# RWKV recurrence with a gated convolution behind it: plan lengths as measured, and stores from a buffer of their own

## The chip, the cores and the metric

The kernel runs on one core of one Trainium2 chip. The metric is the device time of one execution in microseconds; lower is better.

## The reference

The first half is a recurrence over 768 steps for 4 batches and 8 heads, with a 40 x 40 state each. The second half takes its output as 320 channels, runs a causal convolution of 5 taps, a sigmoid gate and two 320 x 320 matrix products. Everything is float32.

```python
for t in range(S):                                   # S = 768
    y[:, :, t] = einsum('bhd,bhde->bhe', r_t, state)
    Sa = einsum('bhde,bhe->bhd', state, a_t)
    state = state * w_t[:, :, None, :] - einsum('bhd,bhe->bhde', Sa, b_t) \
            + einsum('bhd,bhe->bhde', v_t, k_t)
x = y.transpose(0, 2, 1, 3).reshape(B, S, H * D)     # 4 x 768 x 320
gate = sigmoid(sum_k conv_w[k] * x shifted by 4 - k)
out = (gate * (x @ w_val)) @ w_out
```

## The kernel before

The sequence is cut into 24 chunks of 32 steps. All 32 pairs of batch and head are worked on together, packed into the partitions. A chunk has a part that doesn't need the state and a part that does.

Without the state: load the inputs (`load`), running products of the decay (`scan`, L351), their reciprocals (`ln`, `exp`, `nw0`, `nw1`), scaled inputs (`at`, `kt`), copies with zeros in the other half (`qb`, L380), the products between steps (`am`, L389) and their evacuation (`aev_l`, `aev_k`, L408). Four chunks share one triangular solve on VectorE: `begin`, 60 `step` operations (L443, L445) and `end` (L452); the first four chunks are solved by halves with `q1` and `q2` on TensorE, for which `end2` transposes a block into the tile `td`, and `db` spreads it.

With the state: `u0` (L515, L519), `evac_u0` (L523), `ut` (L528) and `u` (L532), their evacuations on ScalarE (`evac_ut` L536, `evac_u` L540), `g` (L544) and `evac_g` (L547), the output and the new state in PSUM (`ysa`, `ysb`, L553), from which `evac_s` (L563) takes the state and `evac_y` (L577) the output. `st` and `kbt` (L419) are transposes.

`evac_y` writes the output into a half of the tile XEW, one half for each pair of chunks in turn. `new_xe` (L572) copies the four steps before the pair into its half; it waits until the half's former content has been moved. From there the second half of the reference is done pair by pair (the last two chunks singly, in tiles that have come free):

- `xd`: twelve small transfers within the chip's memory (L705) that bring channels into the partitions, from xe to a half of the tile XTW, called xt
- `cv`: the convolution, on ScalarE (first tap, L725) and VectorE (L727), into the one tile AG
- `abs`, `gexp`, `gln`, `max`, `gate`: the sigmoid, in AG
- `val` (L90, L98) and `gv` (L757): the value product and its multiplication with the gate, in AG
- `out` (L108): the output product; `os` (L772): its copy from PSUM into the same half of XTW; `store` (L776): the transfer to the output

The order of all this is not written by hand. Each operation is given to a planner as `op(name, engine, length, predecessors, function, delay, ...)`, with length and delay in ns. The delay is the time from the operation's end to when another engine can use its result; for a transfer it stands for the landing. The planner runs a greedy list scheduling forward and backward, several times, ranks operations by how long a chain hangs on each, and keeps the shortest plan. Every engine then gets its instructions in the plan's order, and waits at run time for what each really needs. The plan also decides where TensorE gets matmuls without use (L795) in planned gaps, and which of four PSUM slots a result takes.

The two stores of a pair and its moves are issued by POOL (the very last by SP). The moves wait, in the plan and at run time, for the stores of the pair two before, as these read the same half of XTW.

Of the kernel before, what the change touches and what calls it, by code (L numbers as in the profile page):

```python
# [17 lines left out]
C = 32  # L18
# [26 lines left out]
def ac(n):  # L45
    return 154 + 0.833 * n
# [106 lines left out]
class Plan:  # L153
# [111 lines left out]
def fast_path(ctx, tc, ins, out, nch, cst, wts, wz, wmx):  # L265
# [57 lines left out]
    def B2(nm, c):  # L323
        return (nm, c, 0), (nm, c, 1)
# [62 lines left out]
    def amat(c, s):  # L387
        for j, i in JI:
            T.matmul(out=s[hr(i), j * 64:j * 64 + 64], lhsT=QB[c % NQ][:, pj(j, i)].rearrange("p z t -> p (z t)"),  # L389
                     rhs=st_["kb", c][:, pj(j, i)].rearrange("p x t -> p (x t)"), start=True, stop=True)  # L390
# [24 lines left out]
    def flips(s, src, g, w):  # L415

        for b in range(4):
            u = 8 * g + 2 * b
            T.transpose(out=s[:, b * 128:b * 128 + ER], in_=src[:, u:u + 2].rearrange("p i f -> p (i f)"), identity=ident[0:ER, 0:ER])  # L419
# [38 lines left out]
                        in1=maskL.unsqueeze(1).to_broadcast([128, 8, C]), op=ALU.mult)  # L458

    def end2(g):  # L460
        td = st_["td", g] = ch.tile([128, P16, 4, 8], F32, name="td", bufs=1)
        V.transpose(out=td.rearrange("p s c u -> p (s c u)"), in_=st_["x", g][:, 0:P16].rearrange("p s t -> p (s t)"))

    def nblock(c, z):
# [114 lines left out]
    def slot(nm):  # L579
        return st_["slot", nm]  # L580

    for c in range(nch):
        q = c - NQ
        g, c4 = sof[c]
        op(("load", c), "SP", 4300, ["cst"] * (c == 1) + [(x, c - 3) for x in ("at", "kt", "relu", "scan")], lambda c=c: load(c), 2200)
# [15 lines left out]
        op(am, "PE", 870, [("qb", c, 0), ("qb", c, 1), ("kt", c), ("pre_a", q)] + gg + [("q2", sg[TWO][0] - 1)] * (c == NQ - 1), lambda c=c, n=am: amat(c, slot(n)), give=[("aev_l", c), ("aev_k", c)])  # L601
        op(("aev_l", c), "DVE" if two else "ACT", 480 if two else 604, [am, "cst", ("lz", g)] + gg, lambda c=c, n=am: aev_l(c, slot(n)))
        op(("aev_k", c), "DVE", 440, [am, ("pre_a", q)], lambda c=c, n=am: aev_k(c, slot(n)))
        op(("pre_a", c), "DVE", dv(512), [("aev_k", c), "cst", ("u0", c - 2)], lambda c=c: pre_a(c))
        for k in range(2):
            kt = ("kbt", c, k)
            op(kt, "PE", 430, [("kt", c), "cst", *B2("ysb", q)] + ([("q1", sg[TWO][0] - 2), ("q1", sg[TWO][0] - 1)] if NQ - 2 <= c < NQ else []), lambda c=c, k=k, n=kt: flips(slot(n), st_["kb", c].rearrange("p u x t -> p u (x t)"), k, 128), give=[("kbe", c, k)])
# [26 lines left out]
        op(("load2", c), "SP", 2500, [("load", 4 + c)] * (c < 2) + [*B2("ysb", c - 2), ("u0", c - 2)], lambda c=c: load2(c), 2200)  # L634
        op(("load3", c), "SP", 3200, [("load2", c)] + [("rs", c - 1), ("rs1", c - 1), ("vs", c - 1), ("es", c - 1)], lambda c=c: load3(c), 2200)
# [5 lines left out]
        op(("u0", c), "PE", 1900 if c else 900, [("pre_a", c), ("qb", c, 0), ("qb", c, 1), ("load2", c), *B2("evac_s", c - 1), *B2("evac_y", c - 1), "pz"], lambda c=c: stage_u0(c))  # L641
# [9 lines left out]
        op(nm, "PE", 960, [("evac_ut", c), ("rs", c), ("rs1", c), ("vs", c)], lambda c=c, n=nm: stage_g(c, slot(n)), give=[("evac_g", c)])  # L651
        op(("evac_g", c), "DVE", dv(512, 1), [nm, "cst", ("load2", c)], lambda c=c, n=nm: evac_g(c, slot(n)))
        fr = [("evac_u", c, 0), ("evac_u", c, 1), ("evac_ut", c)]
        if c:
            for k in range(2):
                op(("ysa", c, k), "PE", 650, fr + [("evac_st", c - 1, k), ("es", c)], lambda c=c, k=k: stage_y(c, k, S2, RE, 40, True, False))
        for k in range(2):
            op(("ysb", c, k), "PE", 650, fr + [("ysa", c, k), ("evac_g", c), ("kbe", c, k)], lambda c=c, k=k: stage_y(c, k, KB[c % NQ], st_["w", c], 64, c == 0, True))
            if c + 1 < nch:
                op(("evac_s", c, k), "DVE", dv(320, 1), [("ysb", c, k), ("u0", c), ("st", c - 1, k), "sz"], lambda c=c, k=k: evac_s(c, k))  # L660
            op(("evac_y", c, k), "DVE", dv(256, 1), [("ysb", c, k), ("xe", gof[c][0])], lambda c=c, k=k: evac_y(c, k))
            if c + 1 < nch:
                nm = ("st", c, k)
                op(nm, "PE", 430, [("evac_s", c, k), "cst", "sz"], lambda c=c, k=k, n=nm: flips(slot(n), ST, k, 104), give=[("evac_st", c, k)])
# [29 lines left out]
    for gi, (c, n) in enumerate(groups):  # L694
# [10 lines left out]
                (nc.sync if last and hf else G).dma_start(out=o, in_=i)  # L705
        last = tail > 0
        mq = ("SP", 860, 650) if last else ("POOL", 560, 850)
        xw = [x for j in range(n) for x in B2("evac_y", c + j)] + wl + [("cv", pg, 4, 0), ("cv", pg, 4, 1), ("cv", pg, 4, 2), ("val", pg, 2), ("store", pg, 0), ("store", pg, 1)]
# [54 lines left out]
        for j in range(n):  # L763
            def outm(j=j, c=c, n=n, gf=gf):
                out_mms(nc, slot(("out", c, j))[:, 0:DM], gf, wo, j, n)
            nm = ("out", c, j)
            op(nm, "PE", 1980, prev_gv + om + ([] if late else [when[3 + j]]), outm, give=[("os", c, j)])
            om = [nm]
            prev_out.append(nm)

            def osc(j=j, c=c, xo=xo):
                A.copy(out=xo[0][:, xo[1] + j * DM:xo[1] + (j + 1) * DM], in_=slot(("out", c, j))[:, 0:DM])  # L772
            op(("os", c, j), "ACT", ac(DM), om, osc)

            def store(j=j, c=c, n=n, L=L, xo=xo, last=last):
                (nc.sync if last else G).dma_start(out=out[j * B // n:(j + 1) * B // n, c * C:c * C + L], in_=xo[0][:, xo[1] + j * DM:xo[1] + (j + 1) * DM])  # L776
# [172 lines left out]
```

## Time and profile before

| | |
|---|---|
| median of 3 runs | 543.69 us (542.23 to 549.13) |
| profiled execution | 543.18 us |
| its span, first to last instruction | 541.3 us |
| time outside the span | 1.9 us |
| busy: TensorE, VectorE, ScalarE, POOL | 423.7, 378.6, 316.1, 103.4 us |
| mean granted TensorE clock | 0.852 |
| read from and written to HBM | 49.25 and 3.93 MB |

In rows of the profile, PE is TensorE, DVE VectorE, ACT ScalarE, POOL GpSimd, and SP the engine that issues loads. A row of the timeline has the start in us, the length, the engine, the line of the program, the operation, output and inputs by the program's names, the shape, how many, and in brackets the idle time of the engine before it with what ended it. A row of the chain has start, length and what was waited for; a row of the list of waits has the total in us, the number of times and the longest.

### The profile page before, as it was taken

Reading aid. Unit: us, or ns where it says so; the run is one execution under the profiler, and the core shown is the slowest. Engines: PE = TensorE matmul, PEld = TensorE weight load, DVE = VectorE, ACT = ScalarE, POOL = GpSimd, SP = SyncE. Lnnn points to the kernel's source line nnn. Section 1 sums busy time; section 2 is a strip of 40 time slices with the busy share of each in tenths; the row PEclk is TensorE's granted clock in tenths of the full one; section 3 lists DMA queues with packets and bytes.
Section 4 is the critical chain, followed back from the end, with each engine's and each line's share of the span. In section 5 each row is a group of like instructions: output and inputs, shape, how many; then the busy total and the mean of one; then the engine's idle time right before and its main releaser. Section 6 shows DMA issues by size and latency. Waiting matters only on the chain.

```text
span 541.3 us, 22177 instructions
## 1 busy us (share of the span) xinstructions
PE 423.7 (78%) x9769; PEld 364.2 (67%) x9769; DVE 378.6 (70%) x935; ACT 316.1 (58%) x644; POOL 103.4 (19%) x187
## 2 busy tenths in 40 slices
PE   4707669879769979897983996985987988998790
PEld 3707669778759768777872876774876766776660
DVE  4548946887999988796994695994795746443430
ACT  3636455657867769685684485676464527562530
POOL 3000000040310140032031023013014051338410
PEclk8766756888869999897996898997999697999696
DMA  8855733474664646647355526441252352341101
GB/s 179 199 134 135 188 85 90 100 172 111 152 152 99 146 118 136 154 112 164 86 130 133 145 49 154 87 113 29 78 105 60 66 124 59 96 90 35 37 17 38
DMA packets 24262, 58.96 MB, mean 109 GB/s; under 512 B 10953, under 2 KB 15215, under 8 KB 21665
## 3 DMA queue, kind: packets, MB, share of 16 engines
q1 hardware_dynamic: 13169, 49.52, 39.1%
q0 software_dynamic: 10992, 7.97, 6.3%
q8 instruction: 78, 1.28, 1.1%
q14 instruction: 23, 0.19, 0.1%
HBM read 49.25 MB, written 3.93 MB: 98 GB/s over the span
## 4 chain that ended last, share of the span: by engine, by line
PE 42%; DMA 18%; issue 17%; DVE 11%; ACT 6%; POOL 5%; POOLq 0%; ACTq 0%; DVEq 0%
DMA out<-xt 6%; PE pf L90 5%; PE pc L553 4%; PE pf L389 4%; DMA xt<-xe 4%; PE pf L108 4%; DMA ew<-in_ew 4%; PE pf L419 4%; PE pc L532 4%; PE pf L544 4%; POOL xt L705 4%; PE pc L515 3%; PE pc L519 3%; PE pc L528 3%; DMA ag<-in_wts 1%
## 5 line engine op out<-in xcount | busy, mean ns | idle before, releaser
L705 POOL DMA_DIRECT2D xt<-xe x132 | 68.0, 521 | 199.9 <-DVE tm L443 113.7
L727 DVE SCALAR_TENSOR_TENSOR ag<-xt,wts,ag 128x256 f32<-128x256 f32 (+1 forms) x132 | 53.6, 431 | 10.7 <-ACT ag L725 10.6
L776 POOL DMA_DIRECT2D out<-xt x22 | 18.2, 827 | 218.7 <-ACT xt L772 211.6
L389 PE MATMUL pf<-kb,qb 104*64 104x64 f32 x768 | 34.8, 260 | 30.7 <-DVE kb L384 22.8
L389 PEld LDWEIGHTS pf<-kb,qb 104*64 104x64 f32 x768 | 31.9, 172 | 33.0 <-ACT er L356 16.0
L445 DVE TENSOR_TENSOR x<-x,tm 128x58 f32<-128x58 f32 (+9 forms) x164 | 51.4, 314 | 0.6
L443 DVE TENSOR_TENSOR tm<-x 128x58 f32<-128x58 f32 (+9 forms) x164 | 51.3, 313 | 0.6
L108 PE MATMUL pf<-wts,ag 128*128 128x320 f32 x132 | 47.6, 482 | 1.0 <-DVE ag L757 1.0
L544 PE MATMUL pf<-rb,vu 104*64 104x64 f32 x768 | 33.0, 248 | 17.6 <-DVE ak L408 12.3
L544 PEld LDWEIGHTS pf<-rb,vu 104*64 104x64 f32 x768 | 29.2, 159 | 22.2 <-DVE ak L408 12.7
L540 ACT COPY w<-pc 32x640 f32<-32x640 f32 x48 | 32.9, 685 | 17.4 <-PE pc L532 16.9
L351 DVE TENSOR_TENSOR_SCAN lam<-ew,ind 104x528 f32<-104x528 f32 x24 | 30.0, 1248 | 16.8 <-DMA ew<-in_ew 16.7
L532 PE MATMUL pc<-ub,T 64*32 64x80 f32 x768 | 37.4, 254 | 5.3 <-issue 5.3
L553 PE MATMUL pc<-re,s 40*40 40x72 f32 x1472 | 33.1, 231 | 8.3 <-ACT s L422 4.6
L523 ACT ACTIVATE ub<-pc,cst 128x320 f32<-128x320 f32 x48 | 22.7, 522 | 28.0 <-PE pc L519 28.0
L532 PEld LDWEIGHTS pc<-ub,T 64*32 64x32 f32 x768 | 31.9, 121 | 7.8 <-issue 6.5
L380 ACT ACTIVATE qb<-qa,cst 104x512 f32<-104x512 f32 x48 | 32.5, 714 | 7.4 <-DVE qa L377 7.3
L503 ACT ACTIVATE rb<-rv,cst 104x512 f32<-104x512 f32 x48 | 34.5, 719 | 1.9 <-DMA rv<-in_rv 1.6
L553 PEld LDWEIGHTS pc<-re,s 40*40 40x40 f32 x1472 | 27.1, 117 | 12.5 <-ACT s L422 5.0
L553 PE MATMUL pc<-w,kbt 64*40 64x72 f32 x1536 | 33.3, 232 | 1.9 <-DVE w L547 1.1
L419 PE MATMUL pf<-cst,kb 104*128 104x104 f32 x192 | 28.7, 290 | 7.2 <-DVE kb L384 4.3
L528 PE MATMUL pc<-T,ub 64*40 64x32 f32 x1536 | 23.5, 212 | 13.1 <-issue 11.9
(119 smaller groups left out, 952.3 us busy)
## 6 DMA issues: line engine op xcount, KB each, us to landing
ew<-in_ew SPq DMA_DIRECT2D x24, 838.5 KB
rv<-in_rv SPq DMA_DIRECT2D x24, 624.0 KB
w<-in_vw SPq DMA_DIRECT2D x48, 144.0 KB
va<-in_va SPq DMA_DIRECT2D x24, 160.0 KB
out<-xt POOLq DMA_DIRECT2D x22, 160.0 KB, 7.0
xt<-xe POOLq DMA_DIRECT2D x66, 42.5 KB, 5.0
ag<-in_wts SPq DMA_DIRECT2D x5, 323.0 KB
re<-in_re SPq DMA_DIRECT2D x1, 468.0 KB
```

The lines of the kernel that those rows point to most:

```text
L108: T.matmul(out=ps, lhsT=gv[r, q * L:q * L + 128], rhs=wo[k][r], start=(k == 0), stop=(k == 2))
L389: T.matmul(out=s[hr(i), j * 64:j * 64 + 64], lhsT=QB[c % NQ][:, pj(j, i)].rearrange("p z t -> p (z t)"), rhs=st_["kb", c][:, pj(j, i)].rea ...
L419: T.transpose(out=s[:, b * 128:b * 128 + ER], in_=src[:, u:u + 2].rearrange("p i f -> p (i f)"), identity=ident[0:ER, 0:ER])
L443: V.tensor_tensor(out=tv, in0=x[:, :, j:j + 1, r].to_broadcast(sh), in1=x[:, :, 0:j, j:j + 1].to_broadcast(sh), op=ALU.mult)
L445: V.tensor_tensor(out=x[:, :, 0:j, r], in0=x[:, :, 0:j, r], in1=tv, op=ALU.subtract)
L503: A.activation(out=st_["rb", c][:, :, z], in_=st_["rv", c][:, 0], func=AF.Copy, scale=ownz[:, z:z + 1])
L528: T.matmul(out=PC[0][hr(z, 40), i, j * C:j * C + C], lhsT=UB[hr(i), j, z], rhs=st_["T", c][hr(i), j], start=True, stop=True)
L532: T.matmul(out=PC[1][i * 64 + 32:i * 64 + 64, j // 4, j % 4 * 80:j % 4 * 80 + 80], lhsT=st_["T", c][hr(i), j], rhs=UB[hr(i), j].rearrange( ...
L544: T.matmul(out=s[hr(i), j * 64:j * 64 + 64], lhsT=st_["vu", c][:, pj(j, i)].rearrange("p x t -> p (x t)"), rhs=st_["rb", c][:, pj(j, i)].r ...
L553: T.matmul(out=PC[g][hr(z, 40), i, j % 4 * 72:j % 4 * 72 + 72], lhsT=l[hr(i, k), j * 2 + z], rhs=rhs[hr(i, k), j * 2 + z], start=start and ...
L705: (nc.sync if last and hf else G).dma_start(out=o, in_=i)
L727: V.scalar_tensor_tensor(out=acc[:, q], in0=xt[:, q, i:i + L], scalar=cw[:, k, i:i + 1], in1=acc[:, q], op0=ALU.mult, op1=ALU.add)
```

## The change

Three things are edited.

Lengths and delays in the plan: matmul groups get other lengths (`am` 870 to 1060 ns, transposes 430 to 510, `u0` 1900 to 2120, `ut` 950 to 750, `u` 1100 to 1240, `g` 960 to 1080, `ysa` and `ysb` 650 to 550 each, `val` 1450 to 1530 and 820 to 950); the delay of loads goes from 2200 to 4000, that of the moves `xd` from 2200 to 5500.

The output has a tile OS of its own for all pairs but the single chunks at the end. The copy into it waits for the store of the pair before, and the moves no longer wait for stores. The tile `td` moves into the first half of XTW, so the first moves wait for its readers.

All stores are issued by ACT, with a planned length of 400 ns.

```diff
+    OS = const.tile([128, 2 * DM], F32, name="os")
...
-        td = st_["td", g] = ch.tile([128, P16, 4, 8], F32, name="td", bufs=1)
+        td = st_["td", g] = XTW[:, 0:512].rearrange("p (s c u) -> p s c u", s=P16, c=4)
...
-        op(("load", c), "SP", 4300, [...], lambda c=c: load(c), 2200)
+        op(("load", c), "SP", 4300, [...], lambda c=c: load(c), 4000)
...
-        op(am, "PE", 870, [...], ...)
+        op(am, "PE", 1060, [...], ...)
...
-        op(("ut", c), "PE", 950, eu, lambda c=c: stage_ut(c))
-        op(("u", c), "PE", 1100, eu, lambda c=c: stage_u(c))
+        op(("ut", c), "PE", 750, eu, lambda c=c: stage_ut(c))
+        op(("u", c), "PE", 1240, eu, lambda c=c: stage_u(c))
...
-        xw = [...] + wl + [("cv", pg, 4, 0), ("cv", pg, 4, 1), ("cv", pg, 4, 2), ("val", pg, 2), ("store", pg, 0), ("store", pg, 1)]
+        xw = [...] + wl + [("cv", pg, 4, 0), ("cv", pg, 4, 1), ("cv", pg, 4, 2), ("val", pg, 2)]
+        if gi == 0:
+            xw += [("db", x, z) for x in range(sg[TWO][0]) for z in range(2)]
+        if gi == 1:
+            xw += [("q2", sg[TWO][0] - 1)]
...
-            op(("xd", c, hf), mq[0] if hf else "POOL", (7 * 560, 4 * mq[1])[hf], xw, lambda hf=hf, xd=xd: xd(hf), 2200)
+            op(("xd", c, hf), mq[0] if hf else "POOL", (7 * 560, 4 * mq[1])[hf], xw, lambda hf=hf, xd=xd: xd(hf), 5500)
...
-        xo = (XTW, gi % 2 * 680) if tail < 0 else (fk[tail], 0)
+        xo = (OS, 0) if tail < 0 else (fk[tail], 0)
+        po = groups[gi - 1][0] if gi and tail < 0 else -1
...
-            op(("os", c, j), "ACT", ac(DM), om, osc)
+            op(("os", c, j), "ACT", ac(DM), om + [("store", po, j)], osc)
...
-                (nc.sync if last else G).dma_start(out=out[...], in_=xo[0][...])
-            op(("store", c, j), mq[0], mq[2], [("os", c, j)], store, 2200)
+                A.dma_start(out=out[...], in_=xo[0][...])
+            op(("store", c, j), "ACT", 400, [("os", c, j)], store, 2200)
```

More of the change, by code (lines that the diff above doesn't have):

```diff
@@ L584, in fast_path @@
         g, c4 = sof[c]
-        op(("load", c), "SP", 4300, ["cst"] * (c == 1) + [(x, c - 3) for x in ("at", "kt", "relu", "scan")], lambda c=c: load(c), 2200)
+        op(("load", c), "SP", 4300, ["cst"] * (c == 1) + [(x, c - 3) for x in ("at", "kt", "relu", "scan")], lambda c=c: load(c), 4000)
         op(("scan", c), "DVE", 1250, [("load", c), "ind1", *B2("evac_y", c - NL), *B2("evac_s", c - NL)], lambda c=c: scan(c))
@@ L600, in fast_path @@
             op(("lz", g), "DVE", 1080, gg, lambda g=g: lz(g))
-        op(am, "PE", 870, [("qb", c, 0), ("qb", c, 1), ("kt", c), ("pre_a", q)] + gg + [("q2", sg[TWO][0] - 1)] * (c == NQ - 1), lambda c=c, n=am: amat(c, slot(n)), give=[("aev_l", c), ("aev_k", c)])
+        op(am, "PE", 1060, [("qb", c, 0), ("qb", c, 1), ("kt", c), ("pre_a", q)] + gg + [("q2", sg[TWO][0] - 1)] * (c == NQ - 1), lambda c=c, n=am: amat(c, slot(n)), give=[("aev_l", c), ("aev_k", c)])
         op(("aev_l", c), "DVE" if two else "ACT", 480 if two else 604, [am, "cst", ("lz", g)] + gg, lambda c=c, n=am: aev_l(c, slot(n)))
@@ L633, in fast_path @@
             op(("pre_t", c), "DVE", 540, [("end", g), "cst", ("ut", c - 2), ("u", c - 2)], lambda c=c: pre_t(c))
-        op(("load2", c), "SP", 2500, [("load", 4 + c)] * (c < 2) + [*B2("ysb", c - 2), ("u0", c - 2)], lambda c=c: load2(c), 2200)
-        op(("load3", c), "SP", 3200, [("load2", c)] + [("rs", c - 1), ("rs1", c - 1), ("vs", c - 1), ("es", c - 1)], lambda c=c: load3(c), 2200)
+        op(("load2", c), "SP", 2500, [("load", 4 + c)] * (c < 2) + [*B2("ysb", c - 2), ("u0", c - 2)], lambda c=c: load2(c), 4000)
+        op(("load3", c), "SP", 3200, [("load2", c)] + [("rs", c - 1), ("rs1", c - 1), ("vs", c - 1), ("es", c - 1)], lambda c=c: load3(c), 4000)
         op(("rs", c), "ACT", ac(512), [("load3", c), "cst", ("g", c - 2)], lambda c=c: spread_r(c, 0))
@@ L640, in fast_path @@
             op(("es", c), "ACT", ac(512), [("load3", c), "ez", *B2("ysa", c - 1)], lambda c=c: spread_e(c))
-        op(("u0", c), "PE", 1900 if c else 900, [("pre_a", c), ("qb", c, 0), ("qb", c, 1), ("load2", c), *B2("evac_s", c - 1), *B2("evac_y", c - 1), "pz"], lambda c=c: stage_u0(c))
+        op(("u0", c), "PE", 2120 if c else 1060, [("pre_a", c), ("qb", c, 0), ("qb", c, 1), ("load2", c), *B2("evac_s", c - 1), *B2("evac_y", c - 1), "pz"], lambda c=c: stage_u0(c))
         for z in range(2):
@@ L650, in fast_path @@
         nm = ("g", c)
-        op(nm, "PE", 960, [("evac_ut", c), ("rs", c), ("rs1", c), ("vs", c)], lambda c=c, n=nm: stage_g(c, slot(n)), give=[("evac_g", c)])
+        op(nm, "PE", 1080, [("evac_ut", c), ("rs", c), ("rs1", c), ("vs", c)], lambda c=c, n=nm: stage_g(c, slot(n)), give=[("evac_g", c)])
         op(("evac_g", c), "DVE", dv(512, 1), [nm, "cst", ("load2", c)], lambda c=c, n=nm: evac_g(c, slot(n)))
@@ L655, in fast_path @@
             for k in range(2):
-                op(("ysa", c, k), "PE", 650, fr + [("evac_st", c - 1, k), ("es", c)], lambda c=c, k=k: stage_y(c, k, S2, RE, 40, True, False))
+                op(("ysa", c, k), "PE", 550, fr + [("evac_st", c - 1, k), ("es", c)], lambda c=c, k=k: stage_y(c, k, S2, RE, 40, True, False))
         for k in range(2):
-            op(("ysb", c, k), "PE", 650, fr + [("ysa", c, k), ("evac_g", c), ("kbe", c, k)], lambda c=c, k=k: stage_y(c, k, KB[c % NQ], st_["w", c], 64, c == 0, True))
+            op(("ysb", c, k), "PE", 550, fr + [("ysa", c, k), ("evac_g", c), ("kbe", c, k)], lambda c=c, k=k: stage_y(c, k, KB[c % NQ], st_["w", c], 64, c == 0, True))
             if c + 1 < nch:
@@ L663, in fast_path @@
                 nm = ("st", c, k)
-                op(nm, "PE", 430, [("evac_s", c, k), "cst", "sz"], lambda c=c, k=k, n=nm: flips(slot(n), ST, k, 104), give=[("evac_st", c, k)])
+                op(nm, "PE", 510, [("evac_s", c, k), "cst", "sz"], lambda c=c, k=k, n=nm: flips(slot(n), ST, k, 104), give=[("evac_st", c, k)])
                 op(("evac_st", c, k), "ACT", ac(320), [nm, ("ysa", c, k)], lambda c=c, k=k, n=nm: unflip(S2, slot(n), k))
@@ L707, in fast_path @@
         mq = ("SP", 860, 650) if last else ("POOL", 560, 850)
-        xw = [x for j in range(n) for x in B2("evac_y", c + j)] + wl + [("cv", pg, 4, 0), ("cv", pg, 4, 1), ("cv", pg, 4, 2), ("val", pg, 2), ("store", pg, 0), ("store", pg, 1)]
+        xw = [x for j in range(n) for x in B2("evac_y", c + j)] + wl + [("cv", pg, 4, 0), ("cv", pg, 4, 1), ("cv", pg, 4, 2), ("val", pg, 2)]
+        if gi == 0:
+            xw += [("db", x, z) for x in range(sg[TWO][0]) for z in range(2)]
+        if gi == 1:
+            xw += [("q2", sg[TWO][0] - 1)]
         if tail >= 0:
@@ L751, in val @@
                 val_mms(nc, slot(("val", c, m))[:, 0:vx[m]], wv, xt, m, L)
-            op(("val", c, m), "PE", (1450 if m < 2 else 820) * f, xds + wl + vm + ([] if late else gates + [when[m]]), val, give=[("gv", c, m)])
+            op(("val", c, m), "PE", (1530 if m < 2 else 950) * f, xds + wl + vm + ([] if late else gates + [when[m]]), val, give=[("gv", c, m)])
             vm = [("val", c, m)]
@@ L772, in osc @@
                 A.copy(out=xo[0][:, xo[1] + j * DM:xo[1] + (j + 1) * DM], in_=slot(("out", c, j))[:, 0:DM])
-            op(("os", c, j), "ACT", ac(DM), om, osc)
+            op(("os", c, j), "ACT", ac(DM), om + [("store", po, j)], osc)
             def store(j=j, c=c, n=n, L=L, xo=xo, last=last):
-                (nc.sync if last else G).dma_start(out=out[j * B // n:(j + 1) * B // n, c * C:c * C + L], in_=xo[0][:, xo[1] + j * DM:xo[1] + (j + 1) * DM])
-            op(("store", c, j), mq[0], mq[2], [("os", c, j)], store, 2200)
+                A.dma_start(out=out[j * B // n:(j + 1) * B // n, c * C:c * C + L], in_=xo[0][:, xo[1] + j * DM:xo[1] + (j + 1) * DM])
+            op(("store", c, j), "ACT", 400, [("os", c, j)], store, 2200)
     A.preload_act_table_set("natural_log_exp_and_others")
```

2 lines of the change are left out of this document (1 added, 1 removed).

## The prediction

> **What bounds the kernel now.** I read the page first: engines, slices, chain.
>
> ```profile
> PE 423.7 (78%) x9769; PEld 364.2 (67%) x9769; DVE 378.6 (70%) x935; ACT 316.1 (58%) x644; POOL 103.4 (19%) x187
> PE   4707669879769979897983996985987988998790
> PEclk8766756888869999897996898997999697999696
> PE 42%; DMA 18%; issue 17%; DVE 11%; ACT 6%; POOL 5%; POOLq 0%; ACTq 0%; DVEq 0%
> ```
>
> No engine is full. PE leads with 78%, and its slices show holes: the 22nd has 3 tenths busy, and the granted clock (the row PEclk) dips around the holes. The chain gives 18% of the span to DMA, although only loads and small moves are transferred. So I looked for transfers on which an engine waits inside the loop. I call the pair of chunks that begins with chunk c "pair c"; xd(c) is its twelve moves from the result tile xe to the gate's input xt. The list of waits and the chain in order of time around the worst hole:
>
> ```profile
> DVE xe L572 <- DMA xt<-xe: 19.0, 5, 7.8
> ...
> 272.22 0.43 ACT xt L772
> ...
> 272.94 8.29 DMA out<-xt
> 281.30 0.52 issue
> 281.84 6.63 DMA xt<-xe
> 288.47 0.28 issue
> 288.75 6.62 DMA xt<-xe
> ```
>
> The 22 us from 272.94 on are three transfers in a row: a store of pair 4 (its copy is L772), then the moves of pair 8 that had to wait for it. The timeline of POOL and then that of DVE at the same place:
>
> ```profile
> 272.94 0.83 POOL L776 DMA_DIRECT2D out<-xt  x1 [2.98 <-ACT xt L772]
> 276.25 1.58 POOL L705 DMA_DIRECT2D xt<-xe  x3 [2.48 <-DVE x L445]
> 281.84 4.10 POOL L705 DMA_DIRECT2D xt<-xe  x8 [4.00 <-DMA out<-xt]
> 288.75 0.51 POOL L705 DMA_DIRECT2D xt<-xe  x1 [2.81 <-DMA xt<-xe]
> 264.88 0.28 DVE L757 TENSOR_TENSOR ag<-pf,ag 128x128 f32<-128x128 f32 x1
> 295.44 0.20 DVE L572 COPY xe<-xe 104x64 f32<-104x64 f32 x1 [7.84 <-DMA xt<-xe]
> 371.95 0.19 DVE L572 COPY xe<-xe 104x64 f32<-104x64 f32 x1 [4.82 <-DMA xt<-xe]
> 415.22 0.19 DVE L572 COPY xe<-xe 104x64 f32<-104x64 f32 x1 [3.86 <-DMA xt<-xe]
> ```
>
> The mechanism: the output of pair 4 is copied into the same half of XTW from which its gate was computed, and pair 8 needs that half. Three of its moves touch only columns of the first store (272 of 320); the fourth touches the second store's and waits for its landing. The new edge of xe (L572) then waits for xd, since xe has two halves as well. DVE stands 7.84 us with everything queued behind L572. The same wait occurs five times, 19.0 us in all; the three large ones are shown. In the plan, the store lands 2.2 us after its issue, and so does a move. What PE lost there, from PE's timeline, with one undisturbed run of the same lines first, and ACT's wait before the last:
>
> ```profile
> 271.96 1.15 PE L544 MATMUL pf<-rb,vu 104*64 104x64 f32 x32
> 283.29 1.15 PE L389 MATMUL pf<-kb,qb 104*64 104x64 f32 x32 [1.18 <-ACT qb L380]
> 298.78 1.97 PE L544 MATMUL pf<-rb,vu 104*64 104x64 f32 x32 [6.89 <-DVE ak L408]
> 300.54 3.15 PE L389 MATMUL pf<-kb,qb 104*64 104x64 f32 x64
> 373.65 1.98 PE L544 MATMUL pf<-rb,vu 104*64 104x64 f32 x32 [5.39 <-DVE ak L408]
> 415.66 0.80 PE L108 MATMUL pf<-wts,ag 64*128 64x320 f32 x2 [0.96 <-DVE ag L757]
> 418.30 1.35 PE L515 MATMUL pc<-va,akb 64*64 64x40 f32 x32 [1.83 <-DVE xe L577]
> 448.85 1.97 PE L544 MATMUL pf<-rb,vu 104*64 104x64 f32 x32 [3.33 <-ACT vu L536]
> 445.77 0.51 ACT L725 ACTIVATE ag<-xt,wts 128x256 f32<-128x256 f32 x1 [3.88 <-DMA xt<-xe]
> ```
>
> The idle time in brackets is what PE lost to late moves: behind DVE at three places, and behind ACT, whose L725 reads the moved xt, at the fourth. The first matmuls after each long hole are also slow, 1.97 us where the same 32 take 1.15.
>
> **The change part by part.**
>
> *Outputs with a buffer of their own.* xd no longer waits for the stores, only for the convolution and the value matmuls of the pair two before. The last reader of xt for pair 4 is the group whose product ends at 264.88 + 0.28 = 265.2. The moves may then start at 265.2 instead of 276.25, and the fourth needs no landing: 16.7 us sooner than 281.84. Twelve issues of about 0.51 us, the observed 2.81 us wait of the last one, and a landing of 6.6 us end at about 281. DVE arrives at L572 at 295.44 - 7.84 = 287.6: the wait is gone with 6 us to spare. The other pairs have the same pattern (store, three moves, a wait, nine moves), so I take all the listed holes as gone: 6.89 + 5.39 + 0.96 + 1.83 + 3.33 = **-18.4 us**. The two short waits of DVE (19.0 less the three shown, 2.5 us) show no hole on PE, and I count nothing for them; what could be late next is the convolution, below. Bounds: half of it, -9, if the next wait of each place stands close behind; -23 if the short ones and the fourth's ACT stall count fully.
>
> *The slow start after a hole.* L544 loses 0.82 us, and L389 takes 3.15 for 64 where twice 1.15 is 2.30, so 0.85: 1.7 us a hole. For the three holes over 3 us that is 5.0; I take **-4**, since some other hole may stand there; bounds 0 and -5. The Trainium skill (TensorE: Matmul & The Clock Gate, Part 1: The HAM clock gate) says that an idle window of some 3.4 us puts the array to half rate until it has been busy as long again. By that page the hole of 3.33 us would just escape, and two holes would make 3.4 us, an estimate. Here the run behind the hole of 3.33 us is as slow, 1.97 us, as behind the others.
>
> *Stores on ACT.* POOL loses 23 issues, which hid beside its idle time (19% busy): nothing. SP's single store shows what ACT has to take over:
>
> ```profile
> L776 POOL DMA_DIRECT2D out<-xt x22: 813/827/846, 183.0 to 524.7; - x22
> L776 SPq DMA_DIRECT2D out<-kbt x1: 629/629/629, 528.3 to 528.3; - x1
> DMA to landing us min/median/max: 5.8/6.9/10.3
> ```
>
> With SP's one, ACT issues 24: 24 x 0.63 = 15.1 us, where the plan counts 24 x 0.40. The trace has no store on ACT; SP's row is the nearest. Besides, the store waits for the copy just ahead of it (0.43 us), so the copy no longer overlaps its successor. Queued behind it on ACT are the spreads and evacuations of u0, u and ut, for which PE waits. ACT is idle 42% of the time, so I put three tenths of it on the path: **+4.5**; bounds 0 and 24 x (0.63 + 0.43) = 25.4. The copy into OS now waits for the store of the pair before: a landing of at most 10.3 us, while the closest such stores, those of pairs 18 and 20 below, are issued 19.8 us apart: no wait. A store that lands no sooner costs nothing, save at the end:
>
> ```profile
> 497.52 0.82 POOL L776 DMA_DIRECT2D out<-xt  x1
> 517.28 0.83 POOL L776 DMA_DIRECT2D out<-xt  x1 [3.45 <-ACT xt L772]
> 526.66 0.71 POOL L776 DMA_DIRECT2D out<-kbt  x1 [1.10 <-ACT kbt L772]
> 528.30 0.63 SPq L776 DMA_DIRECT2D out<-kbt  x1
> 534.83 0.20 DVE L814 TENSOR_REDUCE wm<-wmx 104x1 f32<-104x48 f32 x1 [11.67 <-DMA out<-kbt]
> ```
>
> The last store, from SP, holds L814 until 6.5 us after its issue, and POOL's median landing was 6.9; I count 0, bounds -1 and +1. The Trainium skill (DMA: Bandwidth & Descriptors, Issuing engines are not separate DMA queues) says that all queues run on the same sixteen DMA engines and that another issuer saves only issue time. By that rule the second half of the change would bring nothing; the landings here agree, and my gain comes from the dropped wait instead.
>
> *Lengths and delays.* They change only the order in which each engine gets its work. New lengths come closer to the trace (ut: 64 matmuls, planned 0.95, now 0.75):
>
> ```profile
> 267.98 0.81 PE L528 MATMUL pc<-T,ub 64*40 64x32 f32 x64
> PE pc L528 <- issue: 11.9, 5, 2.9
> ```
>
> Delays of 5.5 instead of 2.2 for a move, against the 6.63 above, put the readers of xt and L572 later in the order, which guards the saving. But every op may change place. I take **0**, bounds -10 and +12, from what one chunk loses or wins when its order is lucky: the worst hole alone, with its slow start, cost 6.89 + 1.7 = 8.6. The start (loads, first triangular solve) gets other delays too; it lies in these bounds. PE's stops in the middle of L528, for which the profile shows no releaser, stay (11.9 us). td moves into the first half of XTW, free then: 0.
>
> *Sum.* -18.4 - 4 + 4.5 = -17.9, against the profiled execution of 543.2 us: 525.3. The median of the runs is 543.69, 0.5 more, so I predict **525.8**.
>
> **The rivals.**
>
> *The accumulator takes over from xt.* One tile AG holds the gate and its product, and the next pair's convolution begins as the product before it ends:
>
> ```profile
> 266.82 0.47 DVE L727 SCALAR_TENSOR_TENSOR ag<-xt,wts,ag 128x256 f32<-128x256 f32 x1
> ```
>
> That is 1.7 us after the product's end at 265.2, though the xt it reads had long landed. If that cycle, and not xt, sets the pace, the faster recurrence runs into late moves again towards the end: against it stand the 16.7 us by which the moves come sooner; for it, that the recurrence gains 18 us on them. Half of -22.4 comes back: 543.7 - 11.2 + 4.5 = 537.
>
> *ACT becomes the path (slower).* Place: the two stores of each pair before the evacuations of u and ut. Price: 24 x 1.06 = 25.4 us fully on the path, and beside it the low end of the gain, -9, because the delayed evacuations put DVE's work late where the moves no longer do: 543.7 - 9 + 25.4 = 560. With the full -22.4 it would be 547, so it takes both; against -9 it decides from 0.4 us on the path a store, and passes +2% from 0.8. For it: the plan sees 0.40 and not 0.63. Against it: ACT has 6% of the chain and 58% of the span.
>
> *The new order undoes it.* The change moves the lengths, but the greedy order lands on a worse one: at +12 on top of the forecast with only half of the waits gone, 543.7 - 11.2 + 4.5 + 12 = 549. For it: PE is idle for 541.3 - 423.7 = 117.6 us, and the holes that I have a cause for make 18.4 of them. Against it: the new lengths are nearer to the trace.
>
> *The new order helps too.* At -10 on top: 516; with the upper end of the waits, 511.
>
> **How the numbers follow.** Forecast, 511 to 532: 0.56. Order helps, below 511: 0.07. Accumulator, 532 to 543: 0.17. Order undoes it, 543 to 554: 0.10. ACT, above 554: 0.10. A change of 2% (10.9 us) is about what a measurement can tell from none: faster means under 532.8, so 0.63; within 2%, 0.27; slower, 0.10. The range 506 to 549 leaves out half of the lowest case and the worst seventh: about 0.8 inside.
>
> **What would show it.** In the new profile, L572 should wait for xt<-xe under 5 us in all instead of 19.0; no POOL move should wait for out<-; PE should have no hole over 5 us between 100 and 480 us; ACT should show stores of about 0.6 us and be near 60% busy with its issues. L572 waits that stay, or a convolution still waiting for moves, would say that xt was not the limit. A prologue that moves by more than 5 us, or new holes before L544 and L553 behind ACT, would make the prediction wrong.

## The result

The changed kernel takes 502.25 us (median of 4 runs, 498.02 to 529.18), beside 546.39 us (542.23 to 549.13) for the kernel before. The ratio is 0.917, with a 95% interval of [0.906, 0.928], taken without the runs that stand out as slow, such as that of 529.18 us (granted clock 0.857 instead of 0.888). The profiled execution is 502.78 us with a span of 501.0 us. The forecast was 525.8, its range 506 to 549: the direction was right, the gain more than twice as large as forecast.

The changed kernel's lines stand a few further down: `new_xe` is L573, the moves L706, the convolution L731 and L733, `os` L778, the stores L782. The rows of its page that answer the first four of the prediction (busy times, PE's slices, granted clock, the chain by engine):

```profile
PE 416.8 (83%) x9797; PEld 359.0 (72%) x9797; DVE 378.4 (76%) x935; ACT 314.3 (63%) x644; POOL 83.6 (17%) x164
PE   5718449996879998799989889989798998999990
PEclk9667767897958998769999889999898998999995
PE 63%; DVE 17%; DMA 8%; issue 6%; ACT 3%; SPq 1%; ACTq 0%; DVEq 0%
```

The hole at the 22nd slice is gone, and so are most dips of the clock in the second half. PE has 63% of the chain instead of 42%, transfers 8% instead of 18%. Three answers of the trace of the changed kernel say what became of the waits: the list of waits, POOL's timeline at pair 8, and what is known of L573 and L782 (durations in ns as minimum, median, maximum, then first and last start; ACTq and SPq are the DMA issues of ACT and SP).

```profile
POOL xt L706 <- DMA xt<-xe: 11.1, 5, 4.7
DVE wm L820 <- DMA out<-kbt: 12.5, 1, 12.5
```

```profile
251.70 4.05 POOL L706 DMA_DIRECT2D xt<-xe  x8 [14.00 <-DVE x L446]
256.39 2.03 POOL L706 DMA_DIRECT2D xt<-xe  x4 [0.64 <-DMA xt<-xe]
```

```profile
L573 DVE COPY xe<-xe x12: 175/194/313, 108.6 to 451.0; 104x64 f32<-104x64 f32 x12
L782 ACTq DMA_DIRECT2D out<-os x22: 521/522/1153, 181.5 to 484.3; - x22
L782 ACTq DMA_DIRECT2D out<-kbt x2: 558/567/576, 486.2 to 488.1; - x2
```

The waits have no row in which L573 waits for a transfer, where L572 stood 19.0 us, and none in which a move waits for a store. The moves of pair 8 are issued from 251.70 to 258.42, where before they ran from 276.25 to 289.26.

Where the gain lies shows when the span is cut at the end of the last chunk's `evac_y` in each part. The first chunk is done at 92.1 us instead of 97.3, chunks 1 to 11 take 181.1 instead of 180.7, chunks 12 to 23 take 192.3 instead of 230.1, and what follows takes 35.5 instead of 33.2. So nearly all comes out of the second half of the loop, after the sixth pair. That stretch in both kernels, as windows (length, then busy time and count of PE, PEld (TensorE's weight loads), DVE, ACT and POOL, granted clock, share of DMA, GB/s), before first and then after:

```profile
278.00:508.00 230.00, 186.42 (x4550) 155.87 (x4547) 152.17 (x382) 131.95 (x256) 61.26 (x108) 0.89 0.38 89
```

```profile
273.20:465.50 192.30, 177.13 (x4523) 148.74 (x4522) 147.71 (x372) 125.89 (x248) 45.06 (x86) 0.96 0.41 100
```

The 37.7 us are of two kinds. PE is idle 230.00 - 186.42 = 43.6 us before and 192.30 - 177.13 = 15.2 after: 28.4 us. And it is busy 9.3 us less for about the same matmuls, at a granted clock of 0.96 instead of 0.89.

### The profile page after: what moved, and what is told of

Read it like the earlier page. It is cut to its first block, busy times and chain, and to the rows that moved or that the text cites. A ratio compares the mean times of both kernels' runs of the same rounds, so it can differ in the third digit from the quotient of the medians.

```text
span 501.0 us, 22244 instructions
## 1 busy us (share of the span) xinstructions
PE 416.8 (83%) x9797; PEld 359.0 (72%) x9797; DVE 378.4 (76%) x935; ACT 314.3 (63%) x644; POOL 83.6 (17%) x164
## 4 chain that ended last, share of the span: by engine, by line
PE 63%; DVE 17%; DMA 8%; issue 6%; ACT 3%; SPq 1%; ACTq 0%; DVEq 0%
PE pc L554 10%; PE pf L108 8%; PE pf L90 7%; PE pc L533 6%; PE pf L420 5%; PE pf L545 5%; PE pc L520 5%; PE pc L516 5%; PE pf L390 4%; PE pc L529 3%; DMA w<-in_vw 3%; DMA ew<-in_ew 3%; PE pf L98 2%; DVE lam L352 2%; DVE ag L733 2%
## 5 line engine op out<-in xcount | busy, mean ns | idle before, releaser
L706 POOL DMA_DIRECT2D xt<-xe x132 | 67.2, 515 | 375.5 <-DVE xe L578 132.9
L733 DVE SCALAR_TENSOR_TENSOR ag<-xt,wts,ag 128x256 f32<-128x256 f32 (+1 forms) x132 | 53.2, 433 | 0.2 <-ACT ag L731 0.2
L108 PE MATMUL pf<-wts,ag 128*128 128x320 f32 x132 | 45.8, 469 | 0.0
L352 DVE TENSOR_TENSOR_SCAN lam<-ew,ind 104x528 f32<-104x528 f32 x24 | 30.0, 1249 | 16.8 <-DMA ew<-in_ew 16.8
L554 PE MATMUL pc<-w,kbt 64*40 64x72 f32 x1536 | 35.1, 235 | 4.5 <-issue 4.4
L545 PE MATMUL pf<-rb,vu 104*64 104x64 f32 x768 | 30.7, 236 | 7.8 <-issue 5.0
L533 PE MATMUL pc<-ub,T 64*32 64x80 f32 x768 | 34.9, 245 | 2.6 <-issue 2.6
L545 PEld LDWEIGHTS pf<-rb,vu 104*64 104x64 f32 x768 | 26.9, 148 | 11.2 <-issue 5.8
L554 PEld LDWEIGHTS pc<-w,kbt 64*40 64x40 f32 x1536 | 29.9, 121 | 6.7 <-issue 5.6
L564 DVE TENSOR_TENSOR st<-pc,lam 104x320 f32<-104x320 f32 x46 | 22.1, 484 | 16.5 <-PE pc L554 16.2
L801 PE MATMUL pf<-dm 128*128 128x128 f32 x188 | 32.3, 339 | 2.2 <-ACT kbt L423 1.1
L108 PEld LDWEIGHTS pf<-wts,ag 128*128 128x128 f32 x132 | 21.9, 192 | 15.3 <-issue 7.8
L533 PEld LDWEIGHTS pc<-ub,T 64*32 64x32 f32 x768 | 29.9, 115 | 3.8 <-issue 2.8
```

The lines of the kernel that those rows point to most:

```text
L108: T.matmul(out=ps, lhsT=gv[r, q * L:q * L + 128], rhs=wo[k][r], start=(k == 0), stop=(k == 2))
L352: V.tensor_tensor_scan(out=lam.rearrange("p u t -> p (u t)"), data0=st_["ew", c][:, 0:NW], data1=ind.rearrange("p u t -> p (u t)"), initia ...
L533: T.matmul(out=PC[1][i * 64 + 32:i * 64 + 64, j // 4, j % 4 * 80:j % 4 * 80 + 80], lhsT=st_["T", c][hr(i), j], rhs=UB[hr(i), j].rearrange( ...
L545: T.matmul(out=s[hr(i), j * 64:j * 64 + 64], lhsT=st_["vu", c][:, pj(j, i)].rearrange("p x t -> p (x t)"), rhs=st_["rb", c][:, pj(j, i)].r ...
L554: T.matmul(out=PC[g][hr(z, 40), i, j % 4 * 72:j % 4 * 72 + 72], lhsT=l[hr(i, k), j * 2 + z], rhs=rhs[hr(i, k), j * 2 + z], start=start and ...
L733: V.scalar_tensor_tensor(out=acc[:, q], in0=xt[:, q, i:i + L], scalar=cw[:, k, i:i + 1], in1=acc[:, q], op0=ALU.mult, op1=ALU.add)
```

## The experiments

Theory A: the moves waited for stores and new edges for moves; that chain was the whole gain, and the slow clock behind the holes came along with it. Rival B: the new lengths and delays make a better order, and the stores matter little. Rival C: stores off POOL save POOL's time. Ratios are against the kernel before in the same set.

**The buffer alone, in the old order.** Only the tile is changed at run time; plan, order and issuers stay.

```diff
+    OS = const.tile([128, 2 * DM], F32, name="os")
-        xo = (XTW, gi % 2 * 680) if tail < 0 else (fk[tail], 0)
+        xo = (OS, 0) if tail < 0 else (fk[tail], 0)
```

> Only the copies go into OS (td shares XTW) and the moves need no landed store; the plan is computed as before, so every engine gets the same instructions in the same order, stores on POOL. Theory 'waits' (the time was lost in moves that wait for stores): POOL still issues the second store ahead of the moves, but the landing of 6 to 10 us is gone; L572 waits for xt<-xe under 6 us in all instead of 19.0, time 522 to 533. Theory 'order' (the new plan's order brought it): under 10 us gained, 535 to 546.

Measured: 528.59 us, ratio 0.977 [0.970, 0.984]. The time lies in the range expected of the waits, but L573 still waits 9.9 us instead of under 6, and it is under a third of the whole gain, where A would have most of it. The waits of this kernel, then POOL's timeline at pair 8:

```profile
POOL xt L706 <- DMA out<-os: 21.8, 6, 6.0
POOL xt L706 <- DMA xt<-xe: 17.7, 11, 3.4
DVE xe L573 <- DMA xt<-xe: 9.9, 3, 3.9
```

```profile
270.73 0.83 POOL L777 DMA_DIRECT2D out<-os  x1 [24.75 <-ACT os L773]
274.54 0.82 POOL L777 DMA_DIRECT2D out<-os  x1 [2.98 <-DVE tm L444]
275.35 3.61 POOL L706 DMA_DIRECT2D xt<-xe  x7
282.42 0.51 POOL L706 DMA_DIRECT2D xt<-xe  x1 [3.45 <-DMA out<-os]
```

A move still waits for a store, though they share no data any more. Behind the first store, one store and seven moves are issued; the eighth move stops until the store has landed. In the records of this trace POOL's transfers report to eight completion semaphores in turn (numbers 111 to 118); the ninth transfer, at 282.42, has the same one as the store at 274.54, number 116, so it waits for it. All six waits of 21.8 us in the first row are of this kind. The prediction had not seen this: a buffer alone leaves half of L573's wait.

**Buffer and stores on ACT, in the old order.** As above, and

```diff
-                (nc.sync if last else G).dma_start(out=..., in_=xo[0][...])
+                A.dma_start(out=..., in_=xo[0][...])
```

> As the kernel with OS alone, and the stores are issued by ACT at the places where POOL had them in the plan as before. Theory 'waits': moves free of stores altogether, L572 waits under 3 us, time 520 to 530, within 5 us of the kernel with OS alone, since ACT pays about 0.63 us a store with three tenths of it on the path. Theory 'ACT on the path': 10 to 25 us slower than OS alone. Theory 'order': 535 to 546.

> The old order with OS and ACT stores, as reference on the same chip for the three kernels with VectorE held: 500 to 510.

Measured: 506.61 us, 0.937 [0.931, 0.944], faster than any of the three theories had it; a second time, on another chip, 506.25 us, 0.931 [0.926, 0.936]. Taking the stores off POOL is worth 528.59 - 506.61 = 22.0 us in this order. In its waits L573 has no row, and no move waits for a store. POOL's timeline at pair 8, a row of its page, and the stretch of chunks 12 to 23:

```profile
263.99 4.05 POOL L706 DMA_DIRECT2D xt<-xe  x8 [30.41 <-DVE st L564]
270.58 2.03 POOL L706 DMA_DIRECT2D xt<-xe  x4 [2.54 <-DVE tm L444]
```

```profile
PE 409.6 (81%) x9769; PEld 352.4 (69%) x9769; DVE 378.8 (75%) x935; ACT 315.4 (62%) x644; POOL 83.5 (16%) x164
```

```profile
279.40:476.00 196.60, 176.72 (x4550) 148.47 (x4546) 152.06 (x382) 130.56 (x256) 43.95 (x84) 0.97 0.43 102
```

The moves of pair 8 begin at 263.99 instead of 275.35, and the last four at 270.58 instead of 283.84. Only 3.45 us of that was the shared semaphore. The larger part is POOL's order: with the buffer alone POOL still issued the moves behind the two stores, and these waited for their copies (24.75 us ahead of 270.73).

This is the cleanest comparison of the study: every engine has the order of before, save that the stores sit on ACT, and the stretch has the same 4550 matmul records. It takes 196.6 us instead of 230.0: 23.7 us less idle (43.6 to 19.9), and 9.7 us less busy at clock 0.97 instead of 0.89. So the mechanism without any new order is worth most of the result.

**Lengths and delays alone.** The kernel before with the new numbers in `op(...)` only; stores stay in xt and on POOL.

> The kernel before with the new lengths and delays alone; buffer, waits and stores as before. Theory 'waits': the moves still need landed stores, only better planned; 533 to 545. Theory 'order': most of the 42 us, 505 to 520.

Measured: 509.68 us, 0.941 [0.934, 0.948], as the theory of the order had it. Waits and the stretch of chunks 12 to 23:

```profile
POOL xt L705 <- DMA out<-xt: 6.9, 1, 6.9
DVE xe L572 <- DMA xt<-xe: 4.2, 1, 4.2
DVE xe L572 <- issue: 6.6, 2, 5.7
ACT ag L725 <- DMA xt<-xe: 8.2, 5, 5.0
```

```profile
274.00:470.00 196.00, 177.78 (x4550) 149.06 (x4549) 150.00 (x377) 129.95 (x256) 58.45 (x105) 0.95 0.46 105
```

B holds as well: the new order alone takes the same 34 us out of the same stretch. It doesn't remove the waits, though. L572 stands 4.2 us for moves and 6.6 us more in two stops for which the profile shows no releaser, instead of 19.0 us, and ScalarE's L725 waits 8.2 us for moves, where it was 6.5 before. So the order loses less by late moves; whether by shorter waits or by other work beside them isn't shown. The two halves of the change gain in the same place, and do not add.

**Stores alone, planned with the old lengths.** The changed kernel with the lengths and delays of before.

> The changed kernel with the old lengths and delays: OS, ACT stores and their new dependences in the plan. Theory 'waits': 515 to 528. Theory 'order' (lengths and delays): 533 to 546. If both parts are needed, each alone gives less than 20 us.

Measured: 525.66 us, 0.970 [0.962, 0.978], 3% worse than the new tile and ACT stores in the untouched order. The old lengths with the new tile give another plan. Its chunks 12 to 23 take 192.3 us, as in the changed kernel; the loss lies in chunks 1 to 11, which take 203.0 us instead of some 181. A row of this kernel's waits, PE's stops without a releaser ahead of L554, 8 times, of which 14.3 us lie in chunks 1 to 11:

```profile
PE pc L554 <- issue: 18.1, 8, 4.5
```

The order can thus undo almost half of the gain, as one rival had it, but only with the old lengths.

**Stops of VectorE put back.** The second kernel above (stores on ACT, old order) with VectorE held ahead of five `new_xe`, meant to last as long as it had waited there (19.0 us). The holds came out a quarter longer, 23.7 us:

```diff
+            for _ in range({10: 2, 12: 20, 16: 12, 18: 10, 23: 4}.get(c, 0)):
+                V.tensor_reduce(out=hold, in_=cst[:, 0:NCST], axis=AX.X, op=ALU.max)
```

and, as a control, the same reductions spread, one before each `scan` and each `kt`.

> The kernel in the old order with OS and ACT stores (506.6 us), and VectorE held in front of the five L572 that waited before, by reductions without use of about 2 x 0.4, 20 x 0.4, 12 x 0.4, 10 x 0.4 and 4 x 0.4 us, as long as it waited there (19.0 us). Theory 'L572 with the slow clock': most of the 34 us return, 528 to 540. Theory 'L572 without the clock', the sizing of the prediction: 19 to 21 return, 520 to 528. Theory 'late moves for the convolution and its tail': L572 is a small part, 510 to 519.

> The reference with VectorE held at the five L572, in all 48 reductions of 0.49 us, 23.7 us: 15 to 21 us over the reference, as before. In its profile the slow clock carries most of it (half-rate time up by 30 us or more), PE's idle time under 8.

> The reference with as many reductions (47), one before each scan (L352) but the first and one before each kt (L385): the same 23 us on VectorE without a long stop. Theory 'long stops put the clock to half rate': under 9 us over the reference, half-rate time as in it. Theory 'VectorE's time is what counts': 15 to 21 us over the reference, like the concentrated holds.

Measured: 529.43 us, 0.970 [0.957, 0.982], and again 523.15 us, 0.964 [0.959, 0.969]; spread, 508.82 us, 0.933 [0.928, 0.939], beside 0.931 without reductions on that chip. The groups of the first, VectorE's and PE's timelines behind the longest stop, and its stretch of chunks 12 to 23:

```profile
L575 DVE TENSOR_REDUCE hold<-cst 128x1 f32<-128x326 f32 x48 | 23.7, 493 | 1.4
```

```profile
287.07 10.53 DVE L575 TENSOR_REDUCE hold<-cst 128x1 f32<-128x326 f32 x20
300.84 1.97 PE L546 MATMUL pf<-rb,vu 104*64 104x64 f32 x32 [9.60 <-DVE ak L410]
```

```profile
278.40:494.00 215.60, 184.47 (x4476) 154.79 (x4480) 171.68 (x423) 129.51 (x252) 44.10 (x84) 0.89 0.38 92
```

On the same chip, 23.7 us of VectorE in five stops cost 523.15 - 506.25 = 16.9 us; by the ratios it is 0.033 both times. Nearly the same work in small pieces costs 2.6 us. So it is stops that are dear, not VectorE's time. Beside the kernel without stops the stretch is 19.0 us longer, 11.3 of it idle PE and 7.8 PE busy longer (with 74 fewer records), at clock 0.89 instead of 0.97. A stop thus costs idle time and slower matmuls; that the slow clock would carry most of it, with PE's idle time under 8 us, was not so.

The stops bring back about half of what the freed moves had gained, and only in one place. Chunks 12 to 19, then chunks 20 to 23, of the kernel before, of the one with ACT stores, and of the one with the stops:

```profile
278.00:437.30 159.30, 128.45 (x3130) 108.98 (x3128) 119.06 (x296) 93.87 (x183) 31.32 (x56) 0.88 0.41 95
437.30:508.10 70.80, 58.07 (x1426) 46.99 (x1423) 33.21 (x88) 38.08 (x73) 30.04 (x52) 0.90 0.32 76
279.40:419.80 140.40, 122.45 (x3125) 104.29 (x3120) 118.97 (x296) 93.52 (x183) 24.29 (x48) 0.95 0.46 108
419.80:476.10 56.30, 54.37 (x1430) 44.28 (x1429) 33.19 (x88) 37.14 (x73) 19.65 (x36) 1.00 0.36 88
278.40:440.20 161.80, 132.39 (x3122) 112.62 (x3124) 138.85 (x337) 93.85 (x182) 24.83 (x49) 0.85 0.39 95
440.20:495.40 55.20, 53.48 (x1409) 43.47 (x1406) 34.16 (x90) 37.00 (x73) 19.48 (x37) 1.00 0.33 82
```

In chunks 12 to 19 the freed moves gave 18.9 us, and the stops take all of it back. In chunks 20 to 23 they gave 14.5 us, of which nothing comes back: there the late moves held up ScalarE's first tap (L725) rather than L572: in the kernel before L725 waits 13.2 us for moves in these chunks, L572 1.5. These waits shrank with the moves freed, but no experiment puts them back.

**The same stops with PE kept busy.** The kernel with the stops, and 30 and 22 matmuls without use ahead of `g` in chunks 12 and 16. They write into a PSUM bank that is in use, so part of the output is changed.

```diff
+        for _ in range({12: 30, 16: 22}.get(c, 0)):
+            T.matmul(out=PC[0][:, 0, 384:512], lhsT=dm, rhs=dm, start=True, stop=True, skip_group_check=True)
```

> The concentrated holds, and 30 and 22 matmuls without use put before g of chunks 12 and 16, where PE stood behind the two longest holds. Theory 'the clock multiplies the stop': the matmuls keep the rate up and 4 to 9 us come back against the concentrated holds. Theory 'the stop alone costs': as the concentrated holds or slower.

Measured: 529.59 us, 0.973 [0.968, 0.978], 6.4 us slower than with the bare stops on the same chip. PE's timeline around the two places:

```profile
296.49 9.15 PE L546 MATMUL pc<-dm 128*128 128x128 f32 x60
380.89 1.15 PE L548 MATMUL pf<-rb,vu 104*64 104x64 f32 x32 [1.57 <-DVE ak L410]
```

At the second place the 32 matmuls behind the stop take 1.15 us, as undisturbed ones do, and chunks 12 to 19 take 155.8 us, beside 161.8 with bare stops and 140.4 without any. But the chunks before, which the matmuls don't touch, ended 4.2 us later, and the kernel as a whole is no faster. In all it settles nothing: the rate can be kept, and whether that gains time stays open.

**The changed kernel, varied.** All of these are edits of the changed kernel. Its own repetition in the second of these sets was 503.48 us, 0.930 [0.918, 0.942].

> The changed kernel once more, so that the kernels of this set have it on the same chip: both theories 498 to 510, ratio 0.91 to 0.93.

Each store as two issues of half the columns, to weigh an issue on ACT:

> The changed kernel with each ACT store cut into two issues of half the columns: 24 more issues on ACT. Theory 'ACT on the path for three tenths': 24 x 0.63 x 0.3, 4 to 6 us slower than the changed kernel (506 to 509). Theory 'ACT's issues are hidden': within 2 us of it (500 to 504).

> The kernel with cut ACT stores again, on the same chip as the changed kernel. Theory 'ACT's issues are on the path': 2 to 3% slower than the changed kernel, as the two ratios from two chips suggest (0.943 and 0.917). Theory 'hidden, the rest was the slow clock of that chip': within 1%.

Measured: 515.83 us, 0.943 [0.933, 0.953], and 511.65 us, 0.946 [0.934, 0.958], the second beside the repetition. 24 more issues cost 511.65 - 503.48 = 8.2 us by the medians, but the intervals of the second and the repetition overlap.

Stores on POOL, and on SP, planned there (the other lines as changed):

```diff
-            op(("store", c, j), "ACT", 400, [("os", c, j)], store, 2200)
+            op(("store", c, j), mq[0], mq[2], [("os", c, j)], store, 2200)   # POOL
+            op(("store", c, j), "SP", 650, [("os", c, j)], store, 2200)     # SP
```

> The changed kernel with its stores on POOL (planned at 0.85 us there), buffer and lengths and delays as changed. Theory 'POOL's queue matters' (stores hold the moves behind them, also through the eight completion semaphores that POOL's transfers share): 4 to 15 us slower than the changed kernel. Theory 'ACT's issues cost': 3 to 14 us faster. Theory 'neither': within 3 us.

> The changed kernel with its stores planned and issued on SP (0.65 us there) instead of ACT. Theory 'ACT's issues are on the path' (24 more of them cost 8 us): 4 to 10 us faster than the changed kernel, ratio 0.90 to 0.92. Theory 'stores hold up SP's loads': 3 to 15 us slower, ratio 0.93 to 0.95.

Measured: on POOL 507.48 us, 0.942 [0.933, 0.952], a little behind the repetition and within the overlap; on SP 514.81 us, 0.944 [0.937, 0.950], with before at 550.58 us in that set. Rival C falls: with a plan that expects late moves, the stores are nearly as well on POOL. On SP the loads queue behind stores that wait for their copies, as a row of SP's waits shows:

```profile
SPq L782 <- ACT os L778: 61.1, 14, 12.7
```

No engine waits longer for a load by it (VectorE's L352 waits 16.8 us for `ew` in both kernels), so why this kernel is no faster isn't shown.

Four kernels test the plan: the old delays of 2200 with the new lengths, a reckoned hand-over between engines of 190 instead of 180 ns (a harmless disturbance of the greedy order), no matmuls without use, and 590 of them instead of 221.

```diff
-LAT = 180
+LAT = 190
-                for _ in range(k):
+                for _ in range(0):
-RHO, CAP, DUM = 0.37, 700, 250
+RHO, CAP, DUM = 0.74, 700, 250
```

> The changed kernel with the old delays of loads and moves (2.2 us), new lengths kept. Theory 'delays' (the readers of moves are put where the moves have landed): back to 515 to 526, as with both old. Theory 'lengths' (PE's order): 500 to 508. Theory 'any other order will do': anywhere between.

> The changed kernel with the delay between engines planned at 190 instead of 180 ns: a change without a meaning of its own, which gives another order. What it moves is what any order may move: I expect up to 8 us either way. If it moves more, the share of lengths and delays can't be told from luck of the order.

> The changed kernel without the matmuls without use (L801, 188 records); order of all else as it is. Theory 'the clock multiplies idle time': windows with PE under about two thirds busy are followed by windows at half rate, so half-rate time grows from about 112 us and the time rises by 8 to 30 us (510 to 532). Theory 'the clock is a small term': within 4 us (498 to 506).

> The changed kernel with more matmuls without use in planned gaps (590 instead of 221 in the program's loop of the plan, by a doubled rate at which the plan lets the activity run down). Theory 'half-rate time is the consequence of idle PE': half-rate time under 100 us instead of 107 to 115 and 3 to 10 us faster. Theory 'they only cost PE time': equal or slower.

Measured: 513.64 us (502.23 to 515.87) with old delays and 518.5 us (508.83 to 523.22) without those matmuls, both without a ratio, as their runs scatter too much: inconclusive. In the profiled run without those matmuls the mean granted clock is 0.901, not lower than the changed kernel's 0.888, so half-rate time did not grow there, as the theory of the clock had it. The disturbed order took 504.3 us, 0.927 [0.913, 0.942], as the repetition, so the result doesn't hang on this one order. More matmuls without use: 515.8 us, 0.944 [0.933, 0.955]. A row of its page:

```profile
PE 436.9 (86%) x10027; PEld 379.5 (75%) x10027; DVE 379.2 (75%) x935; ACT 314.2 (62%) x644; POOL 83.6 (16%) x164
```

The mean clock rose to 0.906 from the changed kernel's 0.888, PE is busy 20.1 us longer, and the time did not fall. A higher clock bought with PE's time was no gain here.

None of these kernels is shown to be faster than the changed one.

## Why the prediction was right in direction and wrong in size

The prediction named the right wait, the moves behind the stores. The sizes in its sum were wrong, and so was the edit to which it credited the release. Three terms failed: the holes (-18.4), the slow start (-4), and the stores on ACT (+4.5). In the old order, chunks 12 to 23 gained 33.4 us where these terms make 17.9.

*Late moves (-18.4): too small.* The mechanism was right: in the old order, with the moves freed, the moves of pair 8 begin at 263.99 (265.2 in the prediction), L573 waits for nothing and the large holes go. Idle PE in chunks 12 to 23 fell by 23.7 us, whatever ACT's stores cost included, where the sum had -18.4 + 4.5 = -13.9. I had priced only the five holes whose brackets name a late move. The chunks in which they lie (12, 16, 18 and 20) gave back 14.8 us of idle time, less than 18.4, because other stops took their place: chunk 12 lost the hole of 6.89 us and got one of 3.21 ahead of L554. Another 8.9 us came from places that I had not priced, 5.9 of it in the last chunk, which took 24.1 us before and 16.0 with the moves freed. Its moves, too, came late, and the waits of before held a row of them:

```profile
ACT kbt L725 <- DMA kbt<-xe: 11.9, 5, 3.5
```

Of the 11.9 us, 6.7 fall in the last chunk; with the moves freed the whole row is 4.8 us.

*Slow start after a hole (-4): too small.* I took it as 1.7 us for each of three holes, from the two rows behind the worst hole. Measured, the same 4550 records took 9.7 us less in this stretch. (Over the whole span it is 423.7 - 409.6 = 14.1 us, but 3.2 of that lie ahead of 98 us, before the first move.) Asking the trace of before for windows at half clock around the holes, and around the stop of the last chunk, would have shown it:

```profile
289.30:303.00 13.70, 5.41 (x110) 5.16 (x111) 4.30 (x8) 4.36 (x9) 0.00 (x0) 0.50 0.51 118
371.20:381.50 10.30, 7.85 (x140) 7.28 (x140) 6.82 (x14) 4.13 (x8) 0.00 (x0) 0.50 0.24 64
419.00:429.30 10.30, 10.30 (x152) 7.71 (x150) 8.06 (x23) 3.97 (x7) 0.00 (x0) 0.50 0.47 98
446.30:453.20 6.90, 4.35 (x40) 3.59 (x40) 5.33 (x15) 5.14 (x10) 0.11 (x1) 0.51 0.12 26
501.00:511.20 10.20, 6.93 (x113) 6.50 (x114) 5.89 (x17) 7.04 (x14) 3.07 (x5) 0.50 0.17 41
```

The clock is at half for 6.9 to 13.7 us at each place, long beyond the rows that I read. PE is busy 34.8 us in these five; half of that, 17.4 us, is what full rate would have saved at most, four times my term. (Not all came back: the kernel with the moves freed has half-rate stretches of its own.) How a stretch begins and ends, in windows of 3.4 us of before around the hole of 3.33 us:

```profile
439.40:442.80 3.40, 3.40 (x92) 2.33 (x92) 0.21 (x1) 1.37 (x3) 2.27 (x5) 1.00 0.79 192
442.80:446.20 3.40, 1.35 (x22) 0.84 (x16) 0.00 (x0) 0.43 (x1) 2.96 (x6) 1.00 0.28 78
446.20:449.60 3.40, 0.75 (x14) 0.75 (x16) 1.73 (x5) 1.86 (x5) 0.21 (x1) 0.52 0.17 20
449.60:453.10 3.50, 3.50 (x31) 2.83 (x28) 3.50 (x12) 3.26 (x7) 0.00 (x0) 0.50 0.09 35
453.10:456.50 3.40, 3.37 (x132) 2.34 (x130) 0.85 (x3) 2.35 (x6) 0.79 (x1) 0.99 0.02 5
```

Here the clock falls after a window with 1.35 us of work and rises after one with 3.50. The Trainium skill (TensorE: Matmul & The Clock Gate, Part 1: The HAM clock gate) has it fall after an idle window of some 3.4 us and rise after a busy one. The length of the windows agrees. The fall came after a window that was not idle. The rise agrees in these rows, but not in the one at 419.00, where PE is busy for all 10.3 us and the clock stays at half. My term was not built on the page, but it took the slow rows to end where I stopped reading.

*Stores on ACT (+4.5): wrong sign.* That POOL loses its stores I had put at nothing, because POOL is seldom busy. It was worth 22.0 us in the old order: the moves stood behind the stores in POOL's order and behind their semaphores, so the buffer alone gave 12.5 us of the 22.4 that I had credited to it with the slow start. The cost on ACT is not seen by itself. An issue measured 0.52 us, not 0.63; the 0.63 was the store of a single chunk, which takes 0.57 on ACT. The doubled issues suggest 8 us for 24, within the bounds of 0 to 25.4 and too uncertain to correct the term. That ACT would become the path is refuted by its chain share, 3%. The prediction's other sentence, that this half of the change would bring nothing, falls with the same 22.0 us: the saving lay in what waits behind a store in its issuer's order, which is not part of a store's own time.

*Order (0).* Within its bounds. On top of the freed moves the new plan gives 0.1 to 2%: the first chunk 5.2 us sooner, chunks 12 to 23 192.3 instead of 196.6 us, the end 2.3 us longer than before. The first chunk comes sooner with new lengths and delays alone as well, at 92.6 us; a prologue that moves by more than 5 us is what the prediction had named as a sign against it. By themselves lengths and delays give 31 us, which I had put at nothing because I took "come closer to the trace" and "guard the saving" for side effects.

*The rest.* The accumulator did not take over: no hole over 5 us is left between 100 and 480 us, as I had asked for; the largest of the changed kernel behind VectorE in the second half, and the largest at all, by PE's timeline:

```profile
119.56 0.48 PE L545 MATMUL pf<-rb,vu 104*64 104x64 f32 x5 [4.17 <-issue]
354.40 1.97 PE L545 MATMUL pf<-rb,vu 104*64 104x64 f32 x32 [2.42 <-DVE ak L409]
```

The last wait for a store was 0 in the sum; it grew from 11.67 to 12.5 us, inside my bound of 1.

Three things stay open: how the new order alone gets its gain, what the late moves cost by way of ScalarE in chunks 20 to 23, and whether the slow busy time could be saved by itself. Two kernels that raised the clock with matmuls without use were not faster.

## What to carry to other kernels

Price a wait inside a loop with the clock windows behind it, not with its idle time alone, and count every move that stands behind the same kind of transfer. When a buffer is split off, look what still stands ahead of the transfers in their issuer's order, and whether they meet in their completion semaphores. Try the run-time edit in the fixed order before a plan is made anew, and give the planner landings as measured: here either took nearly the whole gain, and both together little more.

## What the hardware showed that I had not expected

- Half rate came in units of about 3.4 us (stretches of 6.9, 10.3 and 13.7 us) and lasted two to four of them at holes of 1 to 7 us. In the case shown it set in after a unit in which PE had still been busy 1.35 of 3.4 us, and at 419.00 it lasted three units although PE was busy throughout.
- Nine transfers of POOL in a row are tied together by eight completion semaphores: a move with no shared data waited 3.45 us for a store's landing, and all such waits came to 21.8 us.
- An issue of the same store of a pair took 0.83 us on POOL and 0.52 on ACT and on SP; of a single chunk, 0.71 on POOL, 0.63 on SP and 0.57 on ACT.
